# Moving the products of M and the split of w_out further behind their decodes

## The chip, the cores and the metric

The kernel runs on one core of one Trainium2 chip. The metric is the time of one execution in microseconds (us), measured on the device; the time before is the median of three runs. The trace comes from one execution under the hardware profiler. Its engines are PE (TensorE's matmuls), PEld (TensorE's weight loads), DVE (VectorE), ACT (ScalarE), POOL (GpSimd) and SP (which issues the DMAs). Each engine runs its own instructions in program order and waits where an operand is not ready.

## The reference

Three layers in a row, all float32:

```python
# 1 sliding-window attention, 4 batches x 8 heads x 576 positions x 64
scores = q @ k.T / sqrt(64) + alibi bias, masked to 0 <= i - j < 128
x = softmax(scores) @ v                    # reshaped to 2304 x 512
# 2 soft mixture of experts: 8 experts, 4 slots each, 32 slots in all
logits = x @ phi                           # 2304 x 32
slot_in = softmax(logits, over tokens).T @ x
slot_out[e] = relu(slot_in[e] @ w1[e]) @ w2[e]
y = softmax(logits, over slots) @ slot_out # 2304 x 512
# 3 feed-forward
h = y @ w_in                               # 512 -> 2048
out = maximum(0.01 * h, h) @ w_out         # 2048 -> 512
```

## The kernel before, in words

The change lies in the last stage, layer 3. Here y = c @ slot_out has rank 32, so y @ w_in is computed as c @ M with M = slot_out @ w_in, 32 x 2048. M is made in eight chunks of 256 columns, one for each eighth of w_in; the matching eighth of w_out (256 rows) is the other half of a chunk. Numbers are kept as sums of two rounded parts (fp32r), which is why one product takes three matmuls.

For each chunk c these steps stand in the program:

- **Load**: SP fetches the raw words of the eighth of w_in (line 720) and of w_out (line 725), 1 MB each, into a slot that an earlier decode has read out.
- **Decode** (lines 733 to 763): two ACT instructions and then six DVE instructions, all recorded under line 747: once for w_in, once for w_out.
- **Split of w_out**: two ACT casts and two DVE subtractions, also under line 747, make the rounded part WO1 and the rest WO2. They are called the tail below.
- **Products of M** (lines 926 to 938), in two parts. Part 0 multiplies soT by the decoded w_in (line 930, four matmuls in the order and eight records in the trace) into a partial-sum buffer `ph`, and ACT copies it (line 933). Part 1 sums the four quarters by one matmul (line 935), and ACT (line 937) and DVE (line 938) store M.

The main work is 96 units, each for 384 tokens and 128 of the 2048 columns of h. Unit n is written here with these names:

- **s(n)**: one matmul of M and c into `ph` (line 958). The buffer `ph` exists twice, and the products of M use the same two.
- ACT makes the rounded activation (line 962) and the full one (line 966), and DVE the rest of the two, called L970 after its line.
- **o(n)**: nine matmuls into three accumulators (line 980), three of them with WO2 and three with the result of L970. In the first visit the three that need L970 stand last; later they are the third, sixth and ninth.

The units form eight visits to blocks of tokens. When a block is left before all of the 2048 columns are summed, its accumulators are stored by ACT and DVE copies (line 995) or added to an earlier sum by DVE (line 997), and the accumulators are used again by the next visit. For the units that matter: units 0 to 3 use chunk 0, 4 to 11 chunks 0 and 1, 12 to 23 chunks 1 to 3, 24 to 31 chunks 2 and 3, and 32 to 63 all eight in order, so that chunk 4 is first used by unit 48.

The order is written by a list of times in units. Every step is entered with a position (`at_`), the list is sorted by it, and the instructions are recorded in that order; each engine then sees its own part. s(n) stands at n, L970 at n + 0.375, o(n) at n + min(1.9 + 0.13 n, 3.986). So o(n) stands 1.9 units behind s(n) at first and 3.986 units from unit 17 on. Table `DEC` holds the positions of the two decodes of each chunk. The accumulators of units 2, 3, 10, 11, 22, 23, 30 and 31 are stored behind positions 4.16, 5.29, 13.2, 14.33, 25.99, 26.99, 33.99 and 34.99. A load is issued 0.7 unit behind each decode.

Of the kernel before, what the change touches and what calls it, by code (L numbers as in the profile page):

```python
# [21 lines left out]
def attn_softmoe_ffn(ctx: ExitStack, tc: tile.TileContext, q, k, v, phi, w1, w2, w_in, w_out, cst_in, out):  # L22
# [97 lines left out]
    with tc.manual_schedule():  # L120
# [524 lines left out]
        for b in range(B):  # L645
            for nm, f in batch_parts(b).items():
# [3 lines left out]
                if (b, nm) in TAIL:  # L650
                    y = NG - 1 + XO["N3"] + 1e-3 * (1 + TAIL.index((b, nm)))
                elif b == B - 1:
                    y = H * b + (XO["N3"] + LAST[nm] if nm in LAST else min(YO[nm], 5 + XO["N3"] + 1e-3 * YO[nm]))
                else:
                    y = H * b + min(YO[nm], (12 if nm == "sl" else 2 * H - (EARLY if b == B - 2 else 0)) - 1.001 + XO["N3"] + 1e-5 * YO[nm])
# [21 lines left out]
        y = H * (B - 2) + min(YO["sl"], 12 - 1.001 + XO["N3"] + 1e-5 * YO["sl"])  # L677
# [141 lines left out]
        i, j = divmod(late + NL, 4)  # L819
        k = 0  # L820
        while i < len(units_w):
# [5 lines left out]
            i, j, k = i + 1, 0, k + 1  # L827
# [30 lines left out]
        for g in range(E // 4):  # L858
            p2 = ps.tile([128, DM], F32, tag="pb0", name="pb")
            for fc in range(FC):  # L860
# [7 lines left out]
                i = g * FC + fc  # L868
# [144 lines left out]
        def at_(y, f, *a):  # L1013
            ev.append((y, len(ev), lambda: f(*a)))

        for n, u in enumerate(units):
# [6 lines left out]
            if u[2] == visits[u[0]][3] - 1:  # L1023
                for i in range(3):
# [5 lines left out]
        at_(1.05, keep, WX["h"], wpc)  # L1030
        loads = [(load_wi, 4, "p13"), (load_wo, 4, "a3"), (load_wi, 5, "a2"), (load_wo, 5, "b2"), (load_wi, 6, "p9"),
                 (load_wo, 6, "p0"), (load_wi, 7, "p12"), (load_wo, 7, "p13")]
        DEC = {1: (.45, 3.45), 2: (6.45, 8.45), 3: (11.45, 13.45), 4: (22.45, 25.45), 5: (29.45, 32.45), 6: (36.45, 39.45), 7: (43.45, 46.45)}

        def dec(c, split, y):
            ops = []

            def go(l, i):
                ops.extend(decode(c, split) if not ops else [])
                ops[l][i]()  # L1040
            for i in range(2):
                at_(y - .33 + .01 * i, go, 0, i)
            for i in range(6):
                at_(y + ZO["w"] * i, go, 1, i)
            for i in range(4 if split else 0):
                at_(y + 1.6 + (i // 2), go, 2, i)
            if loads:
                at_(y + .7, *loads.pop(0))
        at_(-.9, *loads.pop(0))
        for c in range(1, NCH):  # L1050
            dec(c, False, DEC[c][0])
            at_(DEC[c][0] + 1.5, emit_M, c, 0)
            at_(DEC[c][0] + 2.5, emit_M, c, 1)
            dec(c, True, DEC[c][1])
        for _, _, f in sorted(ev, key=lambda e: e[:2]):
            f()
# [48 lines left out]
```

## Time and profile before

| | |
|---|---|
| median of 3 runs | 484.15 us (483.93 to 484.27) |
| profiled execution | 484.13 us |
| its span, first to last instruction | 482.4 us |
| mean granted TensorE clock | 0.979 |
| PE busy | 447.8 us, 93% |
| PEld busy | 348.2 us, 72% |
| DVE busy | 288.5 us, 60% |
| ACT busy | 243.1 us, 50% |

The span leaves out 1.7 us of the execution. Attention and the experts fill the span up to about 222 us; the last stage runs from there to the end. A busy share is an average over all of it. The granted clock is a share of full speed: 1.00 stands for 2.4 GHz and 0.50 for 1.2 GHz.

### The profile page before, as it was taken

To read this page: it belongs to the slowest core of one execution; us is meant where nothing else is said; L and a number is where in the kernel's file an instruction comes from. 1 tells how busy PE (TensorE), PEld (TensorE's weight loads), DVE (VectorE), ACT (ScalarE), POOL (GpSimd) and SP (SyncE) were. 2 spreads that over 40 slices of the span, in tenths; PEclk is the share of its full clock that TensorE was granted. 3 is DMA by queue.
4 is the path that set the end of the run, shared out by engine and by line. 5 is a ranking of instruction groups with operands and counts; after the bars stand their busy time and mean duration, and the time that the engine had idled before them with its cause. 6 is when DMAs were issued, how large, how long until landed. Compare 5 with 4: busy or idle time off the path is not lost.

```text
span 482.4 us, 9993 instructions
## 1 busy us (share of the span) xinstructions
PE 447.8 (93%) x3568; PEld 348.2 (72%) x3568; DVE 288.5 (60%) x909; ACT 243.1 (50%) x562; POOL 109.7 (23%) x288
## 2 busy tenths in 40 slices
PE   7897999999999999998987978797979999999996
PEld 7886887887888752435665857575858888888885
DVE  5897999999999550154767547574546223225232
ACT  4675786776777411234756535362634435433330
POOL 3475676566577330200000000000000000000000
PEclk8999999999999999999999999897989999999999
DMA  9249777678578999999734220000000003003011
GB/s 176 77 131 213 206 215 214 186 206 234 163 224 230 302 376 386 391 387 398 275 99 164 88 81 7 1 0 2 0 0 1 0 1 129 2 2 124 8 65 65
DMA packets 66833, 70.30 MB, mean 146 GB/s; under 512 B 23168, under 2 KB 42016, under 8 KB 66784
## 3 DMA queue, kind: packets, MB, share of 16 engines
q1 hardware_dynamic: 66640, 69.53, 45.7%
q8 instruction: 28, 0.46, 0.4%
q14 instruction: 21, 0.17, 0.2%
q10 hardware_dynamic: 144, 0.13, 0.1%
HBM read 64.85 MB, written 4.72 MB: 144 GB/s over the span
## 4 chain that ended last, share of the span: by engine, by line
PE 40%; DVE 8%; ACT 5%; issue 1%; DVEq 0%
PE acc L980 35%; DVE ar L747 5%; PE ph L958 3%; PE ph L930 2%; ACT ar L747 1%; ACT ar L966 1%; ACT p L962 1%; DVE p L970 1%; PE ph L935 1%; DVE ql L997 1%; DVE p L747 0%; ACT p L747 0%; ACT qx L995 0%; ACT b L747 0%; ACT ql L995 0%
## 5 line engine op out<-in xcount | busy, mean ns | idle before, releaser
L980 PE MATMUL acc<-p,p 128*128 128x512 f32 x648 | 163.9, 398 | 1.4 <-DVE qx L997 1.4
L980 PEld LDWEIGHTS acc<-p,p 128*128 128x128 f32 x648 | 122.3, 191 | 28.7 <-DVE qx L997 1.8
L970 DVE TENSOR_TENSOR p<-ar,p 128x384 fp32r<-128x384 f32 x96 | 53.4, 557 | 122.3 <-ACT ar L966 122.2
L962 ACT ACTIVATE p<-ph 128x384 fp32r<-128x384 f32 x96 | 47.4, 494 | 98.1 <-PE ph L958 98.0
L311 DVE CUSTOM_DVE_ANT_0 junk<-sm,ar 128x256 bf16<-128x256 f32 (+2 forms) x160 | 53.6, 375 | 5.8 <-PE sm L301 5.4
L980 PE MATMUL acc<-b,p 128*128 128x512 f32 x216 | 56.7, 408 | 0.3 <-DVE ql L997 0.3
L980 PEld LDWEIGHTS acc<-b,p 128*128 128x128 f32 x216 | 41.2, 194 | 10.3 <-issue 0.8
L350 ACT ACTIVATE ar<-st 128x512 f32<-128x512 f32 x64 | 38.4, 600 | 17.5 <-PE st L343 9.7
L966 ACT ACTIVATE ar<-ph 128x384 f32<-128x384 f32 x96 | 47.0, 489 | 0.0
L342 PE MATMUL st<-kq 128*128 128x256 f32 (+1 forms) x160 | 39.9, 279 | 0.0
L301 PE MATMUL sm<-kb,qb 96*128 96x256 f32 (+2 forms) x160 | 35.5, 316 | 4.1 <-ACT kb L274 2.2
L407 PE MATMUL o_ps<-ar 128*64 128x65 f32 x992 | 38.9, 225 | 0.0
L343 PE MATMUL st<-qb,kb 128*128 128x256 f32 (+1 forms) x160 | 35.8, 270 | 3.2 <-DMA qb<-ms 3.2
L407 PEld LDWEIGHTS o_ps<-ar 128*64 128x64 f32 x992 | 34.8, 138 | 4.1 <-issue 1.5
L958 PE MATMUL ph<-p,p 128*128 128x384 f32 x96 | 32.9, 346 | 0.4 <-DVE p L938 0.3
L274 ACT ACTIVATE qb<-tp 64x288 fp32r<-64x288 f32 x64 | 27.8, 434 | 10.2 <-PE tp L261 8.9
L279 DVE SCALAR_TENSOR_TENSOR kq<-tp,qb 64x288 fp32r<-64x288 f32 x64 | 29.2, 457 | 4.4 <-ACT qb L274 2.5
L343 PEld LDWEIGHTS st<-qb,kb 128*128 128x128 f32 (+1 forms) x160 | 28.6, 179 | 3.8 <-DMA qb<-ms 3.8
L274 ACT ACTIVATE kb<-tp 64x288 fp32r<-64x288 f32 x64 | 28.0, 438 | 6.0 <-PE tp L261 4.7
L281 DVE TENSOR_TENSOR kq<-tp,kb 64x288 fp32r<-64x288 f32 x64 | 29.1, 454 | 1.7
L287 POOL TENSOR_SCALAR_AFFINE_SELECT kq<-qb 64x576 fp32r<-64x576 f32 x32 | 21.2, 662 | 38.3 <-ACT qb L274 32.8
L342 PEld LDWEIGHTS st<-kq 128*128 128x128 f32 (+1 forms) x160 | 28.6, 179 | 1.4 <-issue 0.9
(187 smaller groups left out, 613.1 us busy)
## 6 DMA issues: line engine op xcount, KB each, us to landing
p<-in_moe_w_dram SPq DMA_DIRECT2D x56, 256.0 KB
p<-in_moe_w_dram SPq DMA_DIRECT2D x7, 1024.0 KB
p<-in_moe_w_in_dram SPq DMA_DIRECT2D x5, 1024.0 KB
p<-in_moe_w_out_dram SPq DMA_DIRECT2D x5, 1024.0 KB
ar<-in_k_dram SPq DMA_DIRECT2D x32, 144.0 KB
ar<-in_q_dram SPq DMA_DIRECT2D x32, 144.0 KB
out_dram<-ar SPq DMA_DIRECT2D x17, 256.0 KB
ar<-in_v_dram SPq DMA_DIRECT2D x32, 128.0 KB
```

The costliest lines, as they stand in the source:

```text
L274: nc.scalar.activation(out=b1, in_=pr, func=AF.Copy, scale=2.0 ** (g % H - 2) if half else 1.0)
L301: nc.tensor.matmul(sl, lhsT=Q1[0:MROW, 128 * t:128 * t + mr], rhs=K1[0:MROW, c0:c1], start=True, stop=True)
L311: nc.vector.tensor_tensor_reduce(out=jk[0:mr, 0:n], in0=sl, in1=maskt[0:mr, m0:m0 + n], op0=ALU.add, op1=ALU.max, accum_out=mn[g % 2][0:mr ...
L342: nc.tensor.matmul(sl, lhsT=KX[:, k0:k1], rhs=QA[:, q0:q1], start=True, stop=False)
L343: nc.tensor.matmul(sl, lhsT=kb[g % R][:, k0:k1], rhs=qb[g % R][:, q0:q1], start=False, stop=True)
L350: nc.scalar.activation(out=e, in_=sts.pop((g, s)), func=AF.Exp, scale=2.0 ** -(g % H + 1))
L407: nc.tensor.matmul(o_ps[64 * u:64 * u + 64, t, :], lhsT=lt, rhs=r, start=st, stop=sp, tile_position=(0, 64 * u))
L958: nc.tensor.matmul(p, lhsT=mst[:, 128 * f:128 * f + 128], rhs=rhs, start=True, stop=True)
L962: nc.scalar.activation(out=G[t0, f][0], in_=H1[t0, f], func=AF.Prelu, alpha=0.01)
L966: nc.scalar.activation(out=gg, in_=H1.pop((t0, f)), func=AF.Prelu, alpha=0.01)
L970: nc.vector.tensor_tensor(out=g2, in0=G0.pop((t0, f)), in1=g1.bitcast(F32), op=ALU.subtract)
L980: nc.tensor.matmul(acc[t0][t], lhsT=(g1, g1, g2)[k][:, 128 * t:128 * t + 128], rhs=(WO1, WO2, WO1)[k][c][:, i], start=(f == f0 and k == 0) ...
```

## The change

Three sets of numbers change, and nothing else. Part 0 of a product of M stands 4.5 units behind the position of its w_in decode, from 1.5, and part 1 at 5.5, from 2.5. The tail stands 3.2 and 4.2 units behind its w_out decode, from 1.6 and 2.6. Of the fourteen decode positions three stay, seven move 1 to 3 units ahead (chunks 1, 3, 4 and 5) and four 1 to 2 units back (chunks 6 and 7). Part 0 of the products comes 2 to 5 units later in the program, for chunk 4 alone at the same position (23.95) as before.

```diff
-        DEC = {1: (.45, 3.45), 2: (6.45, 8.45), 3: (11.45, 13.45), 4: (22.45, 25.45), 5: (29.45, 32.45), 6: (36.45, 39.45), 7: (43.45, 46.45)}
+        DEC = {1: (.45, 2.45), 2: (6.45, 8.45), 3: (10.45, 12.45), 4: (19.45, 22.45), 5: (28.45, 31.45), 6: (37.45, 40.45), 7: (45.45, 48.45)}
...
-                at_(y + 1.6 + (i // 2), go, 2, i)
+                at_(y + 3.2 + (i // 2), go, 2, i)
...
-            at_(DEC[c][0] + 1.5, emit_M, c, 0)
-            at_(DEC[c][0] + 2.5, emit_M, c, 1)
+            at_(DEC[c][0] + 4.5, emit_M, c, 0)
+            at_(DEC[c][0] + 5.5, emit_M, c, 1)
```

The first place is PE's queue at chunk 1, before the change. b_3669 and b_3670 are WO1 and WO2 of the first chunks, p_3580 the rounded activations, p_3783 the results of L970, p_3579 and p_3782 the operands c and M of s.

```order
L980 MATMUL acc<-b_3669,p_3580 128x512 x3
L980 MATMUL acc<-b_3670,p_3580 128x512 x3
L980 MATMUL acc<-b_3669,p_3783 128x512 x3
L930 MATMUL ph<-ar 32x256 x4
L958 MATMUL ph<-p_3579,p_3782 128x384
L935 MATMUL ph<-ar,blk 128x256
L958 MATMUL ph<-p_3579,p_3782 128x384
L980 MATMUL acc<-b_3669,p_3580 128x512 x3
```

The same place of the same queue in the changed kernel, from the end of o(0):

```order
L980 MATMUL acc<-b_3669,p_3783 128x512 x3
L958 MATMUL ph<-p_3579,p_3782 128x384 x2
L980 MATMUL acc<-b_3669,p_3580 128x512 x3
L980 MATMUL acc<-b_3670,p_3580 128x512 x3
L980 MATMUL acc<-b_3669,p_3783 128x512 x3
L958 MATMUL ph<-p_3579,p_3782 128x384
L980 MATMUL acc<-b_3669,p_3580 128x512 x3
L980 MATMUL acc<-b_3670,p_3580 128x512 x3
L980 MATMUL acc<-b_3669,p_3783 128x512 x3
L930 MATMUL ph<-ar 32x256 x4
L958 MATMUL ph<-p_3579,p_3782 128x384
```

Before, part 0 of the product stood right behind o(0); now s(2), s(3), o(1), s(4) and o(2) stand ahead of it, and part 1 follows one unit later, behind o(3).

The second place is DVE's queue at chunks 1 and 2, in the changed kernel. The rows of line 747 with b_3680 are the decode of chunk 2's w_in; those that write b_3670 are the tail of chunk 1.

```order
L747 TENSOR_TENSOR b_3670<-ar,b_3669 128x512
L938 TENSOR_TENSOR p_3782<-ph,p_3782 64x256
L970 TENSOR_TENSOR p_3783<-ar,p_3580 128x384
L747 TENSOR_SCALAR ar<-b_3680 128x512 x2
L747 SCALAR_TENSOR_TENSOR ar<-b_3680,ar 128x512
L747 TENSOR_TENSOR b_3670<-ar,b_3669 128x512
L747 SCALAR_TENSOR_TENSOR ar<-b_3680,ar 128x512
L747 SCALAR_TENSOR_TENSOR ar<-ar 128x512 x2
L970 TENSOR_TENSOR p_3783<-ar,p_3580 128x384 x2
```

The L970 in the third row is that of unit 6, the first in the last row that of unit 7. The second subtraction of the tail now stands between the third and the fourth instruction of the next decode; before, both subtractions stood ahead of this decode, each with an L970 behind it.

The third place is DVE's queue where units 22 and 23 end their visit, as the difference from before (-) to now (+). The first two rows are the decode of chunk 4's w_out, those with p_3787 its tail, and those of line 997 add the accumulators.

```order
 L747 SCALAR_TENSOR_TENSOR ar<-ar 128x512 x4
+L970 TENSOR_TENSOR p_3783<-ar,p_3580 128x384 x2
+L938 TENSOR_TENSOR p_3782<-ph,p_3782 64x256
+L970 TENSOR_TENSOR p_3783<-ar,p_3580 128x384
+L747 TENSOR_TENSOR p_3787<-ar,p_3786 128x512
 L997 TENSOR_TENSOR qx<-acc,qx 128x512 x3
 L970 TENSOR_TENSOR p_3783<-ar,p_3580 128x384
+L747 TENSOR_TENSOR p_3787<-ar,p_3786 128x512
 L997 TENSOR_TENSOR ql<-acc,ql 128x512 x3
-L747 TENSOR_TENSOR p_3787<-ar,p_3786 128x512
```

The decode that stood directly ahead of the first three additions is now three L970, one L938 and one subtraction away from them, and each set of three additions has one subtraction of the tail ahead of it.

## Rows read from the trace of the kernel before

**Rows 1.** Waits of PE, 215 to 482: total us, times, longest us.

```profile
PE ph L930 <- DVE ar L747: 16.2, 7, 2.8
PE acc L980 <- DVE qx L997: 1.4, 1, 1.4
...
PE acc L980 <- DVE ql L997: 0.3, 1, 0.3
```

**Rows 2.** Chain of waits at chunk 3's product: start us, us, what.

```profile
256.57 2.48 DVE ar L747 x5
259.19 1.14 PE ph L930 x8
...
260.70 2.10 PE acc L980 x9
262.80 0.43 PE ph L935 x2
```

**Rows 3.** Chain of waits, behind the last three products and near the end.

```profile
308.94 3.85 PE acc L980 x9
...
330.19 1.58 PE ph L930 x8
331.77 4.14 PE acc L980 x9
...
354.33 3.40 PE acc L980 x9
...
465.70 0.17 PE ph L958
465.87 2.07 PE acc L980 x9
...
470.35 8.20 PE acc L980 x36
```

**Rows 4.** Stretches of PE: us, busy us (records), granted clock, DMA share, GB/s.

```profile
281.20:287.20 6.00, 3.56 (x20) 1.00 0.12 11
...
308.90:312.60 3.70, 3.70 (x11) 0.54 0.00 0
...
362.80:470.30 107.50, 107.50 (x482) 1.00 0.10 37
```

**Rows 5.** Timeline of PE: start us, busy us, what, idle before it and releaser.

```profile
225.40 2.48 PE L980 MATMUL acc<-b,p 128*128 128x512 f32 x9
...
230.55 0.44 PE L958 MATMUL ph<-p,p 128*128 128x384 f32 x1
...
231.95 0.45 PE L958 MATMUL ph<-p,p 128*128 128x384 f32 x1 [0.16 <-ACT ar L966]
...
267.78 2.26 PE L980 MATMUL acc<-b,p 128*128 128x512 f32 x9
269.88 0.33 PE L958 MATMUL ph<-p,p 128*128 128x384 f32 x1
```

**Rows 6.** Timeline of DVE.

```profile
229.85 0.56 DVE L970 TENSOR_TENSOR p<-ar,p 128x384 fp32r<-128x384 f32 x1
...
271.16 0.56 DVE L970 TENSOR_TENSOR p<-ar,p 128x384 fp32r<-128x384 f32 x1 [0.87 <-ACT ar L966]
...
283.44 0.76 DVE L747 TENSOR_SCALAR ar<-p 128x512 int32<-128x512 int32 x2
...
286.51 0.55 DVE L970 TENSOR_TENSOR p<-ar,p 128x384 fp32r<-128x384 f32 x1
...
297.59 1.89 DVE L997 TENSOR_TENSOR qx<-acc,qx 128x512 f32<-128x512 f32 x3
```

**Rows 7.** Timeline of ACT.

```profile
237.20 0.59 ACT L995 COPY qx<-acc 128x512 f32<-128x512 f32 x1
237.67 0.64 ACT L747 CAST b<-ar 128x512 fp32r<-128x512 f32 x1
```

**Rows 8.** A stretch of all engines: PE, PEld, DVE, ACT, POOL; clock, DMA, GB/s.

```profile
235.00:245.00 10.00, 8.58 (x38) 6.70 (x36) 8.79 (x18) 7.07 (x16) 0.00 (x0) 1.00 0.35 116
```

## The prediction

> **What bounds the kernel now.** I read three views in this order. The waits of PE over the last stage come first: nearly all of PE's waiting there is seven waits of line 930 (part 0 of a product of M) on DVE's line 747, 16.2 us in all, and two waits of o on the additions of line 997, 1.7 us [rows 1]. Next, the chain of waits shows what such a wait is made of. At chunk 3 the last five DVE instructions of the decode take 2.48 us and part 0 starts 0.14 us behind them [rows 2]: the product stands 1.5 units behind the decode's position, and the decode itself waits on DVE behind an L970 of the unit just begun. PE, in program order, can start nothing of the main work meanwhile. Last, the stretches and the rest of the chain: between 362.8 and 470.3, where no product of M is left, PE is busy all the time at a granted clock of 1.00 [rows 4], one unit every 2.24 us (2.07 for o, 0.17 for s) [rows 3]. So PE is the bound, and the time between 227 and 358 us is this pace plus waits. The reader is to see in [rows 3, 4] that the last three waits cost twice: behind each, PE ran at a lower clock (0.54 in 308.9 to 312.6) and its first o took 3.85, 4.14 and 3.40 us in place of 2.07 to 2.10.
>
> **What the change takes away.**
> - The waits of part 0. It comes 4.5 units behind its decode, at least 4.5 x 2.24 = 10.1 us of PE's work. The decode needs the chain from s to L970, 1.28 us (269.88 to 271.16) [rows 5, 6], and its six DVE instructions, 3.07 us (283.44 to 286.51) [rows 6]. With an L970 (0.56) and a tail subtraction (about 0.63, a third of the 1.89 of three additions of that size [rows 6]) ahead, it is done after 5.5 us. Minus 16.2 us, with 4.6 us to spare.
> - The waits of o on line 997. The changed order has no decode among the L970 and additions at positions 26 and 34. After o(22) ends, three additions take 1.89 us [rows 6]; PE reaches o(24) after two s and one o, 0.17 + 2.07 + 0.17 = 2.41 us. For the second set, a tail subtraction and an L970 stand between: its first addition ends 1.89 + 0.56 + 0.63 + 0.69 = 3.8 us after o(22), and o(25) starts at 2.41 + 2.24 = 4.65. Minus 1.7 us.
> - The refill. An o is busy for 2.26 us, yet the next matmul starts 2.10 us after it (267.78 to 269.88) [rows 5]. Behind a wait this overlap of 0.16 is lost: 9 x 0.16 = 1.4 us.
> - The lower clock. The three o lose 1.75 + 2.04 + 1.33 = 5.1 us against 2.10, 2.10 and 2.07, and the two last L930 0.44 each against 1.14 (1.58; the last read 1.57, so one row stands for both) [rows 2, 3]: 6.0 us.
> - Chunk 1's product put s, part 1 and s next to each other with no o between. From s to s went 1.40 us (230.55 to 231.95) because the second s needed the buffer `ph` that ACT had not read [rows 5]; in flow it is s and part 1, 0.17 + 0.43 [rows 2, 3]. Minus 0.8 us.
>
> Sum: 16.2 + 1.7 + 1.4 + 6.0 + 0.8 = 26.1 us.
>
> Beside this a rule of the Trainium skill bears on the clock: "TensorE: Matmul & The Clock Gate", section "Why this matters for your kernels", has idle gaps between bursts of matmuls put the clock back. The trace agrees only in part: the wait of 2.44 us within 281.2 to 287.2 left the clock at 1.00, that before 308.9 did not [rows 4]. By the rows I count three drops saved; by the rule taken strictly every remaining wait risks one, which is a rival below.
>
> **What it adds.** No instruction is added. What can be late now is L970 behind a decode, in the first units, where o stands only 2 to 3.5 units behind its s. I walked these units in the new order with the durations above and found four places.
> 1. o(1). The decode of chunk 1 stays at 0.45, ahead of L970 of unit 1, which starts at 229.85 and ends at 230.41 as before [rows 6]. PE ends o(0) at about 227.7 (225.40 + 2.48 - 0.16) [rows 5] and no longer has the product to wait for; with two s and six of the nine matmuls (1.40) it stands at 229.45. It waits 1.0 us. Part of the wait of chunk 1 thus only changes its name.
> 2. o(7). After o(3) ends, ACT has eight instructions until unit 6 can go on: two copies, a cast, line 937, two decode steps, 962 and 966. At the 0.47 us from one copy to the next instruction [rows 7] that is 3.8 us. Then DVE has L970 (0.5), the chunk-2 decode with a tail subtraction in its middle (3.07 + 0.63) and the L970 of unit 7 (0.56): 8.5 us. PE reaches the third matmul of o(7) after part 1 (0.43), four s, three o and two matmuls (0.47): 0.43 + 0.68 + 6.30 + 0.47 = 7.9. It waits 0.6 us.
> 3. Chunk 2's product. o(8) stands at 10.94, part 0 at 10.95, o(9) at 12.07, so s(11), part 1 and s(12) stand together, as at chunk 1 before: 0.8 us [rows 5].
> 4. s(13) needs the buffer that line 938 of chunk 2 reads, behind L970 and a tail subtraction: about 0.15 us.
>
> These are 2.6 us, with three refills 3.1 us. Bounds: nothing at all if the walk is pessimistic; above, each of the six decodes of chunks 1 to 3 holding PE for 2 us, two thirds of its 3.07 [rows 6] and twice the wait at o(1): 12 us. I take 3.1, near the low end, because the walk uses measured durations and o falls further behind with each unit.
>
> What stays hidden: the tails (their first use is 2 units or more away, for chunks 4 to 7 10 or more), M itself (chunk 3, the tightest, is stored at 16 and first used by unit 20), and the loads. Those for chunks 3 and 4 are decoded 1 and 3 units earlier, but the DMA engines are only 0.35 busy in 235 to 245 [rows 8], which is before these decodes, and the loads' order is kept.
>
> **Sum.** 26.1 - 3.1 = 23.0 us. A count the other way: 24 o at 2.10, 72 at 2.07 (199.4), 94 s at 0.17 (16.0) and seven products at 1.14 + 0.43 (11.0) [rows 2, 3] are 226.4 us; from 225.40 that ends at 451.8, with the 3.1 at 454.9. Before, the last o ended at 478.55 (470.35 + 8.20) [rows 3]: 23.6 us less. I take 23.3. The profiled execution took 484.13 us, the same as the median of 484.15 within 0.02, so the forecast is 484.1 - 23.3 = **460.8 us**. Its own range is 458 to 464: without the four new waits 457.7, with them doubled 464.
>
> **Rivals.**
> - A: the clock does not come back. What speaks for it: a wait of 2.44 us had no drop and others of the same length had, so the wait alone may not be the cause [rows 1, 4]. Against it: each drop followed a wait, and 107 us of unbroken work stayed at 1.00 [rows 4]. The 6.0 us stay: 466.8 us.
> - B: the early backlog. L970 comes late at each of the six first decodes, not at two: 12 us in place of 3.1, 460.8 + 8.9 = 469.7 us. For it: three decodes now stand within 12 positions of each other with the tails among them. Against it: DVE's work in units 6 to 16 is 4 decodes, 11 L970, 4 subtractions, some 12.3 + 6.2 + 2.5 = 21 us of the 28 that PE needs.
> - C: the rule on the clock. Each of the four new waits lowers the clock as the three old ones did, 2.0 us each: 468.8 us. Against it: these waits are 1.0 us or less, and one of 2.44 did nothing [rows 4].
> - D: slower than before. DVE runs strictly behind PE: an L970 that waits behind a decode delays ACT's 966 three units later (three buffers), this the `ph` buffer, this s, and so the next decode's start. Then all fourteen decodes hold PE for 3.07 us: 43 us, less the 26.1: 501 us. It decides when s to L970, decode and L970 (1.28 + 3.07 + 0.56 = 4.9 us) exceed the distance of o behind s. That distance is 2.0 units (4.6 us) at unit 1, 2.8 (6.3 us) at unit 7 and 3.986 (8.9 us) from unit 17. So only the first units are at risk. The Trainium skill gives the ground for D in "TensorE: Matmul & The Clock Gate", section "Architectural detail: the array is 16× 32×32, not 1× 128×128": VectorE and ScalarE take their instructions strictly first in, first out. The trace agrees: the L970 at 286.51 starts only when the decode's instructions are through [rows 6].
> - E: the change doesn't do what it says: at chunk 4 the product keeps its position, 23.95. But its decode moves 3 units ahead, so the wait there goes too. If one chunk's wait stayed (16.2 / 7 and a refill, 2.5 us), 463.3 us.
>
> **How the numbers follow.** Forecast 0.72, A 0.07, B 0.08, C 0.05, D 0.02, E 0.06. The range is 457.5 to 466.0: from no new wait to just under A, holding the forecast and E and leaving out most of A, B, C and D. Changes of 0.2% (1 us) are about what a measurement can tell here. Faster by more 0.96, within 0.01, slower 0.03: D and what I overlooked.
>
> **What would show it.** Right: line 930 waits for nothing from 232 us on; the clock is 1.00 through the last stage; o runs at 2.24 to 2.27 us from about 265 us to the end; the last o ends near 455. Waits of PE on L970 appear at o(1) and o(7), under 1.5 us each. Wrong: waits of o on L970 beyond unit 16, of s on 966 or 938 at later chunks, a wait of ACT's line 747 on a DMA, or a granted clock under 1.00 behind waits of a microsecond.

## The result and the profile after

The changed kernel takes 457.04 us (median of 4 runs, 455.43 to 458.31) against 484.04 us (480.15 to 484.27) before, a ratio of 0.9458 with a 95% interval of 0.940 to 0.952. The forecast was 460.8 us with a range of 457.5 to 466.0: the direction and the mechanism were right, the gain was forecast too small, and the median lies 0.5 us below the range. The profiled execution took 458.31 us, its span 456.6.

All of the difference lies in the last stage. Below, "the stage" is the time from the start of the first o to the end of the last. Before, it ran from 225.40 to 478.55, 253.15 us; now from 225.64 to 452.76, 227.12 us. That is 26.0 us less, where the steps of the forecast gave 23.0. The profiled time fell by 25.8, since the stage began 0.24 later.

The waits of PE in the changed kernel, with the same columns as [rows 1]:

```profile
PE acc L980 <- DVE p L970: 1.1, 2, 0.8
PE ph L958 <- DVE p L938: 0.3, 1, 0.3
PE ph L930 <- DVE ar L796: 0.2, 1, 0.2
```

The waits of line 930 on line 747 and of o on line 997 are gone. What is left in the stage is the first row, 1.1 us at o(1) and o(7). The other two rows are s(0) and chunk 0's product ahead of the stage, with the same waits as before. The chain of waits at chunk 6 answers to [rows 2, 3]:

```profile
318.87 2.10 PE acc L980 x9
320.97 0.17 PE ph L958
321.14 0.57 PE ph L930 x8
321.71 2.29 PE acc L980 x9
324.01 0.17 PE ph L958
324.18 0.43 PE ph L935 x2
```

The o behind the product takes 2.29 us where it took 4.14. And line 930 takes 0.57 us, half of the 1.14 that [rows 2] show. Three stretches of PE, columns as in [rows 4]:

```profile
235.00:265.00 30.00, 29.36 (x136) 1.00 0.59 206
265.00:340.00 75.00, 75.00 (x349) 1.00 0.04 15
340.00:444.50 104.50, 104.50 (x473) 1.00 0.10 38
```

In the second and third stretch PE has no idle time, and the granted clock is 1.00 in all three. The four places at which the prediction expected new waits, in PE's timeline:

```profile
228.31 1.56 PE L980 MATMUL acc<-b,p 128*128 128x512 f32 x6
230.69 0.96 PE L980 MATMUL acc<-b,p 128*128 128x512 f32 x3 [0.83 <-DVE p L970]
...
244.34 0.63 PE L980 MATMUL acc<-b,p 128*128 128x512 f32 x2
245.20 1.91 PE L980 MATMUL acc<-b,p 128*128 128x512 f32 x7 [0.23 <-DVE p L970]
...
249.87 0.44 PE L958 MATMUL ph<-p,p 128*128 128x384 f32 x1
250.43 0.70 PE L935 MATMUL ph<-ar,blk 128*128 128x256 f32 x2
251.28 0.44 PE L958 MATMUL ph<-p,p 128*128 128x384 f32 x1
...
253.96 0.45 PE L958 MATMUL ph<-p,p 128*128 128x384 f32 x1
```

The first pair is o(1): six matmuls, then the three that need L970. The second is o(7), stopped at its third matmul. The third group is chunk 2's product: 1.41 us from s(11) to s(12), as it was at chunk 1 before [rows 5]. The last row is s(13), 0.3 us late. The prediction had it wait for line 938, and it did not: it starts while line 938 is still running, right behind ACT's line 966.

```profile
253.39 0.51 ACT L966 ACTIVATE ar<-ph 128x384 f32<-128x384 f32 x1
253.81 0.43 DVE L938 TENSOR_TENSOR p<-ph,p 64x256 fp32r<-64x256 f32 x1
```

Why line 930 now takes half is seen in the weight loads. Timeline of PEld around chunk 3's product, before:

```profile
259.16 0.17 PEld L930 LDWEIGHTS ph<-ar 128*32 128x32 f32 x4 [2.92 <-issue]
259.70 0.14 PEld L930 LDWEIGHTS ph<-ar 128*32 128x32 f32 x4 [0.37 <-DVE ar L747]
```

And in the changed kernel:

```profile
258.71 0.16 PEld L930 LDWEIGHTS ph<-ar 128*32 128x32 f32 x8 [0.37 <-ACT ql L995]
```

Before, the first four loads started when the first half of w_in was decoded, and the other four waited again, for the decode's last instruction. The row "1.14 PE ph L930 x8" joined both groups and hid the second wait.

### The profile page after: what moved, and what is told of

Read it like the earlier page. It is cut to its first block, busy times and chain, and to the rows that moved or that the text cites. A ratio compares the mean times of both kernels' runs of the same rounds, so it can differ in the third digit from the quotient of the medians.

```text
span 456.6 us, 9995 instructions
## 1 busy us (share of the span) xinstructions
PE 438.5 (96%) x3568; PEld 344.8 (76%) x3568; DVE 288.2 (63%) x909; ACT 242.9 (53%) x562; POOL 109.3 (24%) x288
## 4 chain that ended last, share of the span: by engine, by line
PE 46%; ACT 2%; DVE 2%; issue 1%; DVEq 0%
PE acc L980 41%; PE ph L958 3%; PE ph L930 1%; DVE ar L747 1%; ACT ar L747 1%; PE ph L935 1%; DVE p L970 0%; ACT ar L966 0%; ACT p L962 0%; ACT ql L995 0%; ACT p L937 0%; PE acc L856 0%; DVE b L747 0%; ACT b L747 0%; ACT p L747 0%
## 5 line engine op out<-in xcount | busy, mean ns | idle before, releaser
L980 PE MATMUL acc<-p,p 128*128 128x512 f32 x648 | 161.0, 393 | 0.0
L980 PEld LDWEIGHTS acc<-p,p 128*128 128x128 f32 x648 | 120.4, 188 | 25.7 <-issue 1.2
L970 DVE TENSOR_TENSOR p<-ar,p 128x384 fp32r<-128x384 f32 x96 | 52.8, 557 | 96.4 <-ACT ar L966 96.4
L980 PE MATMUL acc<-b,p 128*128 128x512 f32 x216 | 55.3, 399 | 1.1 <-DVE p L970 1.1
L980 PEld LDWEIGHTS acc<-b,p 128*128 128x128 f32 x216 | 40.0, 188 | 10.6 <-DVE p L970 2.2
L407 PE MATMUL o_ps<-ar 128*64 128x65 f32 x992 | 39.9, 228 | 0.0
```

The costliest lines, as they stand in the source:

```text
L407: nc.tensor.matmul(o_ps[64 * u:64 * u + 64, t, :], lhsT=lt, rhs=r, start=st, stop=sp, tile_position=(0, 64 * u))
L970: nc.vector.tensor_tensor(out=g2, in0=G0.pop((t0, f)), in1=g1.bitcast(F32), op=ALU.subtract)
L980: nc.tensor.matmul(acc[t0][t], lhsT=(g1, g1, g2)[k][:, 128 * t:128 * t + 128], rhs=(WO1, WO2, WO1)[k][c][:, i], start=(f == f0 and k == 0) ...
```

## The experiments

Each profile is read by the stage, because runs of one kernel differ by some us ahead of it (last section). The medians come from four sessions, in which the kernel before had 481.94 to 484.64. Start, end and length of the stage in us:

| kernel | first o | last o ends | stage | median of its runs |
|---|---|---|---|---|
| before | 225.40 | 478.55 | 253.15 | 484.04 |
| changed | 225.64 | 452.76 | 227.12 | 457.04 |
| changed, again | 225.27 | 452.36 | 227.09 | 455.68 |
| products alone | 224.44 | 454.08 | 229.64 | 458.00 |
| all but products | 221.85 | 473.83 | 251.98 | 480.38 |
| products at 2.5 | 225.24 | 456.51 | 231.27 | 460.81 |
| products at 3.5 | 223.37 | 451.18 | 227.81 | 456.72 |
| old tail | 223.16 | 451.27 | 228.11 | 456.89 |
| late waits | 223.11 | 462.03 | 238.92 | 467.59 (one run) |
| two places | 223.72 | 449.33 | 225.61 | 454.89 |
| chunk 2 alone | 225.42 | 452.48 | 227.06 | 458.01 (one run) |
| chunk 1 alone | 225.60 | 451.25 | 225.65 | 455.72 |
| chunk 1, chunk 2 split | 225.95 | 451.70 | 225.75 | 455.05 |

The theory was: the gain is the waits of line 930 and what follows from them. The rivals: the spacing of the decodes makes it; the clock falls without regard to the waits.

**Products alone.** The kernel before, with

```diff
-            at_(DEC[c][0] + 1.5, emit_M, c, 0)
-            at_(DEC[c][0] + 2.5, emit_M, c, 1)
+            at_(DEC[c][0] + 4.5, emit_M, c, 0)
+            at_(DEC[c][0] + 5.5, emit_M, c, 1)
```

> The kernel before with only the products of M at 4.5 and 5.5 units; decode positions and tails as before. Theory (the waits of line 930 and the lower clock behind them are the gain): line 930 waits under 1 us in all, clock 1.00 through the last stage, the two waits of o on line 997 stay (about 2 us); 458 to 461 us. Rival (the spacing of the decodes makes the gain, the products alone only move the wait): 470 us or more.

Measured: a ratio of 0.945 (0.940 to 0.951); the stage is 23.5 us shorter than before, 90% of the gain. Line 930 waits for no decode. Of o on line 997 only 0.2 us stayed, less than expected. The clock was not at 1.00 throughout: at chunk 2 s waited for ACT, and o behind it was slow.

```profile
251.10 0.69 PE L958 MATMUL ph<-p,p 128*128 128x384 f32 x1 [1.69 <-ACT ar L966]
251.59 3.46 PE L980 MATMUL acc<-b,p 128*128 128x512 f32 x9
```

What held ACT, in its timeline:

```profile
248.29 0.37 ACT L933 COPY ar<-ph 128x256 f32<-128x256 f32 x1 [0.61 <-PE ph L930]
248.56 0.62 ACT L747 CAST p<-ar 128x512 fp32r<-128x512 f32 x1
249.07 0.67 ACT L747 ACTIVATE ar<-p 128x512 f32<-128x512 f32 x1
...
250.56 0.49 ACT L966 ACTIVATE ar<-ph 128x384 f32<-128x384 f32 x1
```

Between line 933 and the 966 that s needed stood a cast of the old tail and the two steps of the next decode, so that 966 came 2.3 us behind 933. The rival's 470 us falls.

**All but the products.** The changed kernel with

```diff
-            at_(DEC[c][0] + 4.5, emit_M, c, 0)
-            at_(DEC[c][0] + 5.5, emit_M, c, 1)
+            at_(DEC[c][0] + 1.5, emit_M, c, 0)
+            at_(DEC[c][0] + 2.5, emit_M, c, 1)
```

> The changed kernel with the products of M back at 1.5 and 2.5 units; new decode positions and tails. Theory: seven waits of line 930 of 2.3 us are back, each with some 0.6 us more hidden inside the row of line 930, and drops of the clock behind the late ones up to 6 us: 476 to 484 us. Rival (decode spacing): under 465 us.

Measured: 480.38 us, a ratio of 0.992 (0.989 to 0.995); the stage is 1.2 us shorter than before. The largest row of PE's waits:

```profile
PE ph L930 <- DVE ar L747: 16.0, 7, 2.4
```

Stretches of PE behind the products of chunks 2, 3, 6 and 7:

```profile
243.30:248.30 5.00, 4.94 (x18) 0.66 0.59 211
256.00:259.00 3.00, 2.96 (x16) 1.00 0.83 270
...
330.20:333.50 3.30, 3.28 (x18) 1.00 0.02 5
...
352.50:357.40 4.90, 4.86 (x18) 0.65 0.00 0
```

The clock fell behind four of the seven waits: chunks 2, 4, 5 and 7, where before it was 5, 6 and 7. So the place in the program doesn't decide it, and not every wait brings it. The gains of the parts don't add: 23.5 and 1.2 alone, 26.0 together, because the new decode positions and tails remove waits that the products' new place brings with it: above all the 1.69 us and the slow o shown above, where the changed kernel's s(12) waits 0.8 us and the o behind it is busy 2.26.

**Products at 2.5 and 3.5.** The changed kernel with

```diff
-            at_(DEC[c][0] + 4.5, emit_M, c, 0)
-            at_(DEC[c][0] + 5.5, emit_M, c, 1)
+            at_(DEC[c][0] + 2.5, emit_M, c, 0)
+            at_(DEC[c][0] + 3.5, emit_M, c, 1)
```

> The changed kernel with the products at 2.5 and 3.5 units. Theory: a decode is done 5.5 us after its position, 2.5 units are 5.6 us, so at chunks 4 to 7 at most 0.5 us of wait is left and the clock stays at 1.00: 457 to 461 us. Rival (the gain is in proportion to the distance): about 472 us.

Measured: 460.81 us (457.66 to 462.05); the stage is 4.2 us longer than with 4.5. The waits ahead of line 930 at chunks 4 to 7 are 0.2 us or none, as expected. Chunk 6, in PE's and in PEld's timeline:

```profile
313.92 0.33 PE L958 MATMUL ph<-p,p 128*128 128x384 f32 x1
...
318.94 1.13 PE L930 MATMUL ph<-ar 128*32 128x256 f32 x8
```

```profile
318.91 0.17 PEld L930 LDWEIGHTS ph<-ar 128*32 128x32 f32 x4 [0.48 <-issue]
319.44 0.14 PEld L930 LDWEIGHTS ph<-ar 128*32 128x32 f32 x4 [0.36 <-DVE ar L747]
```

No wait is shown ahead of line 930, and its row still takes 1.13: the wait for the second half is inside it at all seven chunks, 7 x 0.57 = 4.0 us. The waits ahead add 2.7 (1.43 at chunk 1, 0.62 at chunk 3), and the changed kernel's early waits, 2.2 us, are not here: 4.0 + 2.7 - 2.2 = 4.5, against 4.2 measured. The gain is not in proportion to the distance, and the rival's 472 us falls.

The expectation took 2.5 units for 5.6 us of PE's work. The first row above is the s from which this decode's chain starts. Behind it stand two o and two more s, and then part 0: two units of 2.27 and an s of 0.17, 4.7 us. The second half is ready 5.5 us behind that s (319.44). So one o more ahead of part 0 is needed, which 3.5 units give.

**Products at 3.5 and 4.5.** The same two lines with 3.5 and 4.5.

> The changed kernel with the products at 3.5 and 4.5 units. Theory (the row of line 930 held a wait for the decode's second half, 0.57 us at each of seven products, which ends with the first wait): from chunk 2 on the rows of line 930 read 0.57 to 0.61 us as in the changed kernel, and the stage from the first o to the last stays within 1.5 us of its 227.1. Rival (1.14 us is what the eight matmuls take unless o stands close ahead and behind): 1.1 us at most chunks, the stage 4 us longer.

Measured: 0.57 us at all seven products, a stage of 227.81, 0.7 us longer than with 4.5; two waits of s on line 966, 1.2 us, stand in its early units. Chain of waits at chunk 6:

```profile
317.30 0.57 PE ph L930 x8
317.86 2.29 PE acc L980 x9
```

So 0.57 us is the work, and the rest of 1.14 was waiting. The rival falls.

**Old tail.** The changed kernel with

```diff
-                at_(y + 3.2 + (i // 2), go, 2, i)
+                at_(y + 1.6 + (i // 2), go, 2, i)
```

> The changed kernel with the tails back at 1.6 and 2.6 units. Theory: the tails were on no path that sets the end; within 1.5 us of the changed kernel, 456 to 459.5 us. Rival (a cast of the tail that waits for its decode holds ACT, and so ph and s): 461 us or more, with waits of s on line 966.

Measured: 456.89 us; the stage is 1.0 us longer. Three waits of s on line 966 appeared, 2.0 us in all, as the rival said, at a smaller price than it gave. The longest, in PE's timeline:

```profile
233.07 0.44 PE L958 MATMUL ph<-p,p 128*128 128x384 f32 x1 [1.04 <-ACT ar L966]
```

And what held ACT:

```profile
231.14 0.62 ACT L747 CAST b<-ar 128x512 fp32r<-128x512 f32 x1 [3.10 <-DVE ar L747]
```

ACT idled 3.1 us with the cast at the head of its queue until the first half of its decode was done; 962, a copy and 966 stood behind it, and s waited for 966. The prediction gave the tails no price, since their results are used late. It is their place in ACT's queue that costs. In the whole time this does not show (ratios to the kernel before of 0.944, and 0.946 for the changed kernel).

**Late waits.** The changed kernel, chunks 5 to 7 back at the old distance.

```diff
-            at_(DEC[c][0] + 4.5, emit_M, c, 0)
-            at_(DEC[c][0] + 5.5, emit_M, c, 1)
+            at_(DEC[c][0] + (1.5 if c > 4 else 4.5), emit_M, c, 0)
+            at_(DEC[c][0] + (2.5 if c > 4 else 5.5), emit_M, c, 1)
```

> The changed kernel with the products of chunks 5, 6 and 7 back at 1.5 and 2.5 units; chunks 1 to 4 as changed. Theory: three waits of 2.3 us, 0.57 us inside each row of line 930, and a lower clock behind at least one and up to three, about 2 us each: the stage 10 to 15 us longer than 227.1, and no drop elsewhere. Rival (the clock falls by the place in the program or by chance, not by the wait): 8.5 to 9 us longer and the clock at 1.00 behind all three, or a drop at chunks 1 to 4.

Measured: the stage is 11.8 us longer. PE's timeline at chunks 6 and 7:

```profile
318.69 1.14 PE L930 MATMUL ph<-ar 128*32 128x256 f32 x8 [2.40 <-DVE ar L747]
...
341.01 1.58 PE L930 MATMUL ph<-ar 128*32 128x256 f32 x8 [2.44 <-DVE ar L747]
342.52 3.17 PE L980 MATMUL acc<-p,p 128*128 128x512 f32 x9
```

The stretches behind chunks 5, 6 and 7:

```profile
292.70:297.60 4.90, 4.86 (x18) 0.65 0.00 0
318.60:322.10 3.50, 3.42 (x18) 1.00 0.02 5
341.00:345.60 4.60, 4.59 (x18) 0.64 0.00 0
```

The sum closes: 7.3 us of waits ahead of line 930, 3 x 0.57 = 1.7 inside it, and for the lower clock behind chunks 5 and 7 0.44 each on line 930 and 1.05 and 0.82 on o (3.33 and 3.10 against 2.28 in the chains), 2.75. Together 11.75 of 11.80. The clock fell only behind the waits put in, at two of three. What sets a wait of 2.40 us without a drop apart from one of 2.44 with it stays open.

**Changed again, and two places.** For a better version, two of the four places were moved: chunk 1's decodes one unit later, and chunk 2's product behind o(9).

```diff
-        DEC = {1: (.45, 2.45), ...
+        DEC = {1: (1.45, 3.45), ...
-            at_(DEC[c][0] + 4.5, emit_M, c, 0)
-            at_(DEC[c][0] + 5.5, emit_M, c, 1)
+            at_(DEC[c][0] + {1: 3.5, 2: 6.05}.get(c, 4.5), emit_M, c, 0)
+            at_(DEC[c][0] + {1: 4.5, 2: 7.05}.get(c, 5.5), emit_M, c, 1)
```

> The changed kernel itself, for comparison on one chip with the next: 455 to 459 us.

> The changed kernel with chunk 1's decodes one unit later (1.45 and 3.45, its products at the same place) and chunk 2's products at 12.5 and 13.5, so that an o stands between s(11), part 0, part 1 and the next s. Theory: the wait of o(1) on L970 (0.83 us) and the wait at s(12) (0.8 us) go, that of s(13) on line 938 too (0.3 us); the stage from the first o to the last falls from 227.1 to 225 to 226 us. Rival (what leaves one place is waited for at another, at o(2) or o(7)): 226.5 us or more.

Measured: 455.68 us (453.65 to 457.91) for the changed kernel, 454.89 (452.80 to 455.76) for the other; the stage is 1.5 us shorter. The waits of o(1) and o(7) are gone, but two others came:

```profile
249.55 0.44 PE L958 MATMUL ph<-p,p 128*128 128x384 f32 x1 [0.56 <-ACT ar L966]
...
255.85 0.44 PE L958 MATMUL ph<-p,p 128*128 128x384 f32 x1 [0.49 <-ACT ar L933]
```

**Chunk 2 alone.** Only the entry for chunk 2 of the edit above.

> The changed kernel with chunk 2's products at 12.5 and 13.5 alone. Theory: the wait at s(12) and that of s(13) go, 1.1 us less than 227.1 in the stage; o(1) still waits 0.83 us. Rival: the same wait comes back at s(14) or s(15), 227 us.

Measured: 227.06, nothing gained. s waits for ACT's 966 and 933 instead (0.5 us each): the rival was right here.

**Chunk 1 alone.** Only the entries for chunk 1.

> The changed kernel with chunk 1's decodes at 1.45 and 3.45, products of M in the same places. Theory: o(1) no longer waits on L970 and the tail of chunk 1 leaves the decode ahead of o(7), so that both waits go, 0.83 and 0.23 us with their refills; the stage from the first o to the last falls from 227.1 to 225.5 to 226.0 us. Rival (the two places of the run before helped half each): 226.3 us or more.

Measured: 225.65. All of the 1.5 us is chunk 1's.

**Chunk 1, and chunk 2 split.** With `{1: 3.5, 2: 3.5}` and `{1: 4.5, 2: 6.05}` in the edit of the two places.

> As the run on chunk 1 alone, and chunk 2's part 0 at 9.95, part 1 at 12.5, so that an o stands between any buffer of ph and the next use but one. Theory: also the wait of 0.8 us at s(12) goes, and at most 0.5 us on ACT comes in its place: 224.8 to 225.4 us in the stage; 453 to 456 us in all. Rival (ACT, which has two decode steps, 962, 966 and a cast between, sets s(13) wherever part 1 stands): 225.6 us, as with two places.

Measured: 225.75, no better. PE's timeline at s(13):

```profile
252.52 0.44 PE L958 MATMUL ph<-p,p 128*128 128x384 f32 x1 [0.65 <-ACT ar L966]
```

The rival was right: at all three places tried for the product, s(13) waits for ACT's line 966, 0.3 us in the changed kernel, 0.56 with two places and 0.65 here. In the whole time chunk 1's move can't be told from the changed kernel: 455.72 (454.13 to 456.78) against 455.68, both 0.944 of the kernel before.

## Why the prediction was right, and where it was not

| term of the stage, us | forecast | measured |
|---|---|---|
| waits ahead of line 930 | 16.2 | 16.2 |
| wait inside line 930's rows | 0 | 4.0 |
| waits of o on line 997 | 1.7 | 1.7 |
| lower clock | 6.0 | 5.4 |
| s to s at chunk 1 | 0.8 | 0.8 |
| refill behind waits | 1.4 | none as a term of its own |
| new waits with refills | -3.1 | -2.2 |
| sum | 23.0 | 25.9, of 26.0 |

The errors went both ways. 4.0 us left out and 0.9 too much for the new waits made the forecast too small; 1.4 counted twice and 0.6 too much for the clock made it too large. That it came within 3.8 us of the median is in part luck.

- **The waits.** Right in place and size. Products alone gives 90% of the gain, all but the products next to none. The room for the decode was counted too wide: the new place is not 10.1 us behind the s that starts the chain but four units and an s (9.26 us at chunk 6, 311.88 to 321.14). Against a chain of 5.5 us this changed nothing.
- **The mis-sized term** is the product itself. In the count the other way I took seven products at 1.14 + 0.43 as work that stays. By the weight loads, and by the runs at 2.5 and 3.5 units, part 0 is 0.57 us of work and 0.57 of waiting. The row of the chain merges eight matmuls and shows only the wait ahead of the first. The chain of [rows 2] held the sign: it has five instructions of a decode of six. I read them as the last five; they are the first five, and the sixth ends inside the row of the product. 4.0 us of the gain were missed by this.
- **The clock.** Right that it comes back when the waits go; late waits shows both at once, and rival A (466.8) and rival C (468.8) fall: waits of 0.83 us and less brought no drop, nor did the 1.43 us with the products at 2.5 units. The price, against the o behind a product in the changed kernel (2.28, 2.29 and 2.28), is 1.57 + 1.85 + 1.12 on o and 0.88 on line 930, 5.4. The Trainium skill's rule of "TensorE: Matmul & The Clock Gate", section "Why this matters for your kernels", that idle gaps set the clock back, agrees with the runs in direction. It does not speak of every gap, so rival C, the rule taken strictly, asked more of it than it states; and here drops came behind waits of 1.69 to 2.8 us, shorter than the gaps it names. In before, all but the products and late waits together, 9 of 17 waits of line 930 of 1.6 us or more were followed by a drop.
- **The refill.** The other terms add up to 25.9 of 26.0 us without it. So the overlap that I priced is already in the rows behind a wait; it was counted twice.
- **The new waits.** All four came at the forecast places: o(1) 0.83 (forecast 1.0), o(7) 0.23 (0.6), chunk 2's product 0.8 (0.8), s(13) 0.3 (0.15). For s(13) the reason was wrong: it waited for ACT's line 966, not for line 938. In chunk 1 alone line 938 even starts at 252.9, behind s(13) at 252.46. Rivals B and D fall: beyond unit 16 no o waits for L970. Rival E falls, chunk 4's wait went too.
- **What stays hidden.** For the tails this was wrong in its reason: the old tail costs 1.0 us through ACT's queue.

Of the 3.8 us between forecast and median, the stage makes 2.7 (26.0 in place of 23.3), less 0.2 for its later start; the median lies another 1.3 us below the profiled execution's 458.31.

## What to carry to other kernels

On engines that run in order, put a consumer behind its producer by the whole chain ahead of the producer's last instruction, counted in the work that really stands between them: here 5.5 us, which two o and three s (2.5 units) do not cover and one o more (3.5 units) does. At chunks 4 to 7 nothing is won beyond. Before pricing a merged row as work, look at its parts on the weight-load side: a wait for the second half of an operand hides inside it. And look at what stands behind a waiting instruction in each queue: a cast that waits for its own decode delayed work that had nothing to do with it.

## What the runs showed of the hardware

Waits of 1.69 to 2.8 us brought the clock from 1.00 (2.4 GHz) to the lower level (1.2 GHz) for the first o in some cases and not in others: 2.51 us without a drop (chunk 3 of the kernel before), 1.69 us with one. Two runs of the same kernel agree in the last stage to 0.03 us (227.12 and 227.09), while the start of the stage differs by up to 4 us between kernels that are the same up to there (221.85 to 225.95). The granted clock ahead of the stage goes with it. Over the first 217 us, in the changed kernel, with the products at 3.5 units, and in all but the products:

```profile
0.00:217.00 217.00, 204.74 (x2476) 0.98 0.79 235
```

```profile
0.00:217.00 217.00, 205.75 (x2500) 0.99 0.81 241
```

```profile
0.00:217.00 217.00, 205.54 (x2507) 1.00 0.80 244
```

All thirteen profiles fall into these three groups: eight with 0.98, whose stage starts at 224.44 to 225.95, four with 0.99 at 223.11 to 223.72, and one with 1.00 at 221.85. As an estimate from these rows, 0.01 of 217 us is 2.2 us, about the step between the groups. That the clock there is the cause of the earlier start was not tested.
